# An attention and token-mixer kernel with one fixed order for all engines, a single gelu activation, and plane groups filled by arrival

## The chip, the cores and the metric

The kernel runs on one core of a Trainium2 chip. The metric is the device time of one execution in microseconds (us). A core has engines that run side by side, each through its own list of instructions in order, with semaphores between them: TensorE (PE, matmuls), ScalarE (ACT, activation functions), VectorE (DVE), GpSimd (POOL) and SyncE (SP, which here only issues DMA transfers).

## What is computed

The reference adds three terms over a 2048 x 512 input in bf16:

```python
def _A_ref(x, wqkv, wo):                      # 32 heads of 16 columns
    qkv = ((x @ wqkv).reshape(B, S, 3, H, Dh)).transpose(2, 0, 3, 1, 4)
    q, k, v = qkv[0], qkv[1], qkv[2]
    scores = einsum("bhqd,bhkd->bhqk", q, k) * Dh ** -0.5
    p = softmax(scores, axis=-1)
    o = einsum("bhqk,bhkd->bhqd", p, v)
    return o.transpose(0, 2, 1, 3).reshape(B, S, D) @ wo

def _B_ref(x, w1, b1, w2, b2):                # mixes along the sequence
    h = layernorm(x)
    u = gelu(einsum("bsd,sf->bdf", h, w1) + b1)      # 512 x 1376
    y = einsum("bdf,fs->bds", u, w2) + b2
    return y.transpose(0, 2, 1)

xn = layernorm(x)
return x + _A_ref(xn, ...) + _B_ref(xn, ...)
```

The softmax needs 32 x 2048 x 2048 exponentials, 134 million. They are by far the largest piece of elementwise work.

## The kernel before

**Units.** The attention is cut into 32 blocks (4 blocks of 512 queries by 8 groups of 4 heads). A block has 4 heads, the "rows" r = 0 to 3, and 16 tiles of 128 keys. One head with one key tile is a *unit*: a 128 x 512 tile of scores, 2,048 units in all. A score matmul (`score_mm`, L645) uses a quarter of the PE array's rows, so that up to four scores of four heads run at once into four PSUM banks; such a set is called a *burst*. Seven of the eight PSUM banks hold scores, bank 7 collects the products with V.

**Two ways to the exponential.** An *A unit* is read from PSUM by ScalarE, which computes the exponential (`exp_tile`, L658) over one, two or three neighbouring banks with one instruction, of 512, 1,024 or 1,536 elements for each partition, into a ring of slots (`pT`, and later the space of `wqkv_sb`). A *D unit* is read by VectorE (`dve_first`, L721): it adds a bias to the score as an int16 and clips it, so that the bits of the integer, read as bf16, are a rough power of two. Two shifted copies of these integers, called *planes*, are made by `make_plane` with GpSimd's 64-bit integer add (L730; sometimes with VectorE, L732). The three planes together, weighted, approximate the exponential. An A unit needs one matmul with V (`pv_mm`, L671), a D unit three. Up to four D units of one group lie side by side in one region of 2,048 elements (spare space in `planes`, `x_sb`, `xn_sb`, `xnT` and `w2blk`, whence these names in the profile), and in the kernel before a plane instruction always covers all four places, filled or not, with a place fixed by the row. The program sends 1,378 units by way A and 670 by way D.

**PV matmuls.** They use a quarter of the array's columns each, and up to four of four rows run at once. Below, a *slot* is the time of one such set of up to four matmuls over 512 columns. The QKV, MLP and output projections (L549) have the same form and go in between.

**The rest.** At the end of a block VectorE copies bank 7 out (L1161); for every pair of blocks the denominators go through DRAM to all partitions, with a reciprocal (L1185) and a multiplication (L1204) by VectorE. The token mixer has 11 chains `chain_ut`, one for each 128 columns of w1: 16 matmuls, VectorE's addition of b1 and multiplication by 0.5 (L1058), and then gelu in four steps: square (L1024) and cube (L1028) on VectorE, tanh on ScalarE (L1033), product on VectorE (L1037). Sixteen chains `chain_yo` then multiply with w2 and the output weights. All this is spread over the run between the scores.

**What sets the order.** The order of all engines' instructions is made at build time by a greedy planner: `pe_step` picks the next piece of PE work (a burst, PV matmuls, a step of a chain, or zero matmuls by `z_fill`, L1698) by modelled times of each instruction, `dve_step` and `misc_step` do so for VectorE and GpSimd, and 32 sets of parameters (`STEP_VALUES`), one for each 64 units, steer them. On the chip the order is fixed.

Of the kernel before, what the change touches and what calls it, by code (L numbers as in the profile page):

```python
# [41 lines left out]
def _plane_sum(i):  # L42
    tot = 0.0
    for d, w in zip(SHIFT, WEIGHT):
# [7 lines left out]

DEBUG_SCHED = False
FORM = "P"
N_ZERO0 = 11
N_ZERO1 = 2
N_ZERO2 = 2
NXP = 5
RING_W = 2
W2_POS = 14.2  # L60
DEBUG_CHAINS = False
PLANNED = [0.0]
TUNE0 = dict(even=1, d_end=1, bal=600.0, one_first=False, bal_w=2000.0, lk=0.1, trip=False, marg=60.0, q_max=1400.0, early=0.0, q_lead=1.5, ut=(4.4, 15.28), yo=(15.68, 30.47), d_keep=2, d_last=5, open_pl=2, d_stop=20, w3=1200.0,
            ring_low=4, tol=100.0, lone=800.0, lone_n=2, f_pr=2, f_late=0.2, f_items=3, ring_next=4, pl_next=4, d_slack=120.0,
            pl_open=3, f_bias=0.0, f_early=9.0, s_wait=-1e9, tol2=-1e9, ex2=2.0, ex3=1.0, d_from=1.3, z_cols=3500.0, partial=False, pr_ex=0, dve_planes=6,
            v1=lambda a: (1.2 + 0.8 * a / 16.0, 0.6), v2=lambda a: (2.4 + 1.3 * a / 16.0, 1.6),
            kt=lambda T, c: ((0, 1.0, 2.9, 4.6)[T] + 0.17 * c * (1, 1, 2, 2)[T], (0, 0.5, 2.0, 3.2)[T]))
STEP_KEYS = ("bal", "bal_w", "c_gate", "d_end", "d_from", "d_keep", "d_last", "d_slack", "d_stop", "dve_planes", "early", "even", "ex2", "ex3", "f_bias", "f_early", "f_items", "f_late", "f_pr", "lk", "lone", "lone_n", "marg", "one_first", "open_pl", "partial", "pl_next", "pl_open", "pr_ex", "q_lead", "q_max", "ring_low", "ring_next", "tol", "trip", "z_cols")
STEP_VALUES = (
# [32 lines left out]
)  # L102
STEPS = [dict(zip(STEP_KEYS, v)) for v in STEP_VALUES]
HOOK = [None]
SCORE = (1.05, 0.5, 0.3)
CP_EVERY = 64

GE = "dve"
GELU_C = 0.7978845608028654
NU = 16  # L110
# [1846 lines left out]
```

## Time and profile before

| what | value |
|---|---|
| time, median of 3 runs (lowest to highest) | 671.7 us (671.6 to 671.73) |
| span of the profiled execution (slowest core, the only one) | 670.0 us |
| instructions in the span | 20269 |
| moved by DMA | 30.01 MB |
| DMA queue q1, share of the time of 16 DMA engines | 17.2% |

The profile comes from one execution; its span runs from the first instruction to the last. No total of its own is listed for that execution, so the span is set beside the runs' median. The time of an instruction is the time from its start to its end; neighbours on ScalarE and PE overlap, so the step from one start to the next is shorter than the listed duration, and what an instruction costs its engine is that step.

### The profile page before, as it was taken

Reading aid. Unit: us, or ns where it says so; the run is one execution under the profiler, and the core shown is the slowest. Engines: PE = TensorE matmul, PEld = TensorE weight load, DVE = VectorE, ACT = ScalarE, POOL = GpSimd, SP = SyncE. Lnnn points to the kernel's source line nnn. Section 1 sums busy time; section 2 is a strip of 40 time slices with the busy share of each in tenths; the row PEclk is TensorE's granted clock in tenths of the full one; section 3 lists DMA queues with packets and bytes.
Section 4 is the critical chain, followed back from the end, with each engine's and each line's share of the span. In section 5 each row is a group of like instructions: output and inputs, shape, how many; then the busy total and the mean of one; then the engine's idle time right before and its main releaser. Section 6 shows DMA issues by size and latency. Waiting matters only on the chain.

```text
span 670.0 us, 20269 instructions
## 1 busy us (share of the span) xinstructions
PE 650.3 (97%) x8631; PEld 200.6 (30%) x8631; DVE 582.4 (87%) x970; ACT 654.5 (98%) x830; POOL 490.2 (73%) x511
## 2 busy tenths in 40 slices
PE   8989999999999999999999999999999999999997
PEld 4444333222222222222222222222222223222222
DVE  7886878888998988899888978989898889898895
ACT  6999999999999999999999999999999999999994
POOL 2507558657686779997699786688789678898884
PEclk9999999999999999999999999999999999999999
DMA  7050000201212122010202212122211212211001
GB/s 222 2 109 7 19 20 10 58 12 41 51 38 62 34 50 50 18 42 3 62 26 55 56 45 66 40 48 56 47 35 26 70 31 49 54 41 49 18 21 49
DMA packets 69957, 30.01 MB, mean 45 GB/s; under 512 B 56494, under 2 KB 66734, under 8 KB 69866
## 3 DMA queue, kind: packets, MB, share of 16 engines
q1 hardware_dynamic: 69290, 28.18, 17.2%
q8 instruction: 68, 1.11, 0.7%
q10 hardware_dynamic: 576, 0.52, 0.2%
q14 instruction: 23, 0.19, 0.1%
HBM read 22.15 MB, written 2.61 MB: 37 GB/s over the span
## 4 chain that ended last, share of the span: by engine, by line
ACT 89%; PE 8%; DVE 2%; issue 0%; DVEq 0%
ACT pT L658 64%; ACT wqkv_sb L658 24%; PE ps L645 2%; PE ps L549 2%; PE ps L671 2%; PE ps L555 1%; ACT xres L1033 1%; DVE gT L1037 0%; DVE planes L721 0%; DVE planes L732 0%; PE ps L561 0%; ACT L1033 0%; DVE w2blk L721 0%; ACT mv L517 0%; ACT mv L515 0%
## 5 line engine op out<-in xcount | busy, mean ns | idle before, releaser
L658 ACT ACTIVATE pT<-ps 128x1024 bf16<-128x1024 f32 (+2 forms) x588 | 506.6, 1047 | 1.1 <-PE ps L645 0.7
L645 PE MATMUL ps<-QT,KT 32*128 32x512 bf16 x2048 | 271.5, 384 | 9.6 <-ACT pT L658 4.7
L658 ACT ACTIVATE wqkv_sb<-ps 128x1024 bf16<-128x1024 f32 (+2 forms) x202 | 211.1, 1107 | 0.0
L721 DVE TENSOR_SCALAR planes<-ps 128x512 int16<-128x512 f32 x251 | 165.6, 686 | 23.1 <-PE ps L645 22.2
L721 DVE TENSOR_SCALAR x_sb<-ps 128x512 int16<-128x512 f32 x233 | 154.1, 685 | 24.3 <-PE ps L645 23.5
L671 PE MATMUL ps<-pT,V 128*32 128x512 bf16 x1004 | 169.9, 386 | 1.3 <-DVE V L574 0.8
L645 PEld LDWEIGHTS ps<-QT,KT 32*128 32x128 bf16 x2048 | 75.1, 91 | 270.4 <-ACT pT L658 157.7
L671 PE MATMUL ps<-planes,V 128*32 128x512 bf16 x509 | 93.8, 384 | 0.6 <-DVE planes L732 0.4
L671 PE MATMUL ps<-wqkv_sb,V 128*32 128x512 bf16 x374 | 89.9, 386 | 0.0
L730 POOL INT64_ADD planes<-x_sb x65 | 68.9, 1066 | 26.5 <-DVE x_sb L721 18.2
L721 DVE TENSOR_SCALAR xn_sb<-ps 128x512 int16<-128x512 f32 x99 | 66.1, 686 | 9.3 <-PE ps L645 8.6
L671 PE MATMUL ps<-x_sb,V 128*32 128x512 bf16 x372 | 73.2, 384 | 0.0
L730 POOL INT64_ADD x_sb<-x_sb x41 | 44.1, 1079 | 36.4 <-DVE x_sb L721 33.2
L730 POOL INT64_ADD planes<-planes x56 | 59.6, 1068 | 11.6 <-DVE planes L721 11.5
L730 POOL INT64_ADD x_sb<-planes x49 | 52.4, 1073 | 16.6 <-DVE planes L721 13.7
L671 PE MATMUL ps<-planes,V17b 128*32 128x512 bf16 x251 | 62.2, 384 | 0.0
L671 PE MATMUL ps<-x_sb,V17b 128*32 128x512 bf16 x233 | 60.9, 385 | 0.1
L549 PE MATMUL ps<-xn_sb,w1blk 128*32 128x512 bf16 x688 | 58.4, 383 | 0.2 <-DVE qraw L935 0.2
L549 PE MATMUL ps<-gT,w2blk 128*32 128x512 bf16 (+1 forms) x704 | 57.5, 383 | 0.2 <-ACT pT L658 0.2
L671 PEld LDWEIGHTS ps<-pT,V 128*32 128x32 bf16 x1004 | 43.2, 94 | 46.0 <-issue 35.7
L721 DVE TENSOR_SCALAR xnT<-ps 128x512 int16<-128x512 f32 x65 | 42.7, 684 | 3.5 <-PE ps L645 3.2
L671 PE MATMUL ps<-xn_sb,V 128*32 128x512 bf16 x209 | 44.6, 384 | 0.0
(114 smaller groups left out, 897.3 us busy)
## 6 DMA issues: line engine op xcount, KB each, us to landing
w1blk<-in_B_w_dram SPq DMA_DIRECT2D x10, 512.0 KB, 4.4
w2blk<-in_B_w_dram SPq DMA_DIRECT2D x16, 320.0 KB, 3.4
denb<-rec_scr SPq DMA_DIRECT2D x16, 256.0 KB
xres<-in_A_x_dram SPq DMA_DIRECT2D x16, 128.0 KB, 2.3
QT<-qraw SPq DMA_DIRECT2D x120, 16.0 KB, 1.8
OT<-OT SPq DMA_DIRECT2D x60, 32.0 KB, 2.0
out_dram<-osb SPq DMA_DIRECT2D x13, 128.0 KB, 1.8
x_sb<-in_A_x_dram SPq DMA_DIRECT2D x2, 512.0 KB, 7.1
```

What stands on the lines that cost most here:

```text
L549: op = sc.add("pe", lambda e, sl=sl, c=c: e.matmul(dst[sl, :], lhsT=lhsT[:, sl], rhs=rhs, start=start, stop=stop, tile_position=(0, 32 * c ...
L555: return sc.add("pe", lambda e: e.matmul(bank(bk)[:, 0:n], lhsT=zer[:, 512:640], rhs=zer[:, 0:n], start=True, stop=True), reads=[("zer",)] ...
L645: return sc.add("pe", lambda e: e.matmul(bank(bk), lhsT=KT[32 * r:32 * r + 32, T, 128 * kt:128 * (kt + 1)], rhs=QT[32 * r:32 * r + 32, slo ...
L658: return sc.add("act", lambda e: e.activation(slots(us), pick(ps3, bs), ACTF.Exp, scale=EXP_SCALE), reads=[("bank", b) for b in bs], write ...
L671: return sc.add("pe", lambda e: e.matmul(bank(PV_BANK)[32 * r:32 * r + 32, :], lhsT=vt_[:, off:off + 32], rhs=rhs, start=start, stop=stop, ...
L721: return sc.add("dve", lambda e: e.tensor_scalar(plane_i[pb][:, 512 * r:512 * (r + 1)], bank(bk), BIAS + SHIFT[0], float(SHIFT[0]), ALU.ad ...
L730: return sc.add("pool", lambda e: e.int64_add(plane_q[pb], plane_q[pb0], -down * LANES), reads=rd, writes=wr, name="plane", occ=1015.0, la ...
L1033: return sc.add("act", lambda e: e.activation(gB[0:m, :], gB[0:m, :], ACTF.Tanh, scale=2.0 * GELU_C * GC), reads=kB, writes=kB, occ=t["occ ...
```

## The change

**The order.** The planner, its cost model and its parameters are gone. A text constant, `ORDER`, some 21,400 characters long, lists in one sequence what is issued: `C` the next step of a chain, `S` a burst with its units, banks and, for D units, plane region, `E` an exponential, `F` a D unit's first plane, `L` a further plane, `P` a set of PV matmuls, `Z` zero matmuls, `U` work of the tail. `replay` reads it and adds the instructions to the engines' lists. So how many units go each way, how wide the exponentials are and what stands next to what is now set by the table. Counted from the two programs:

| | before | after |
|---|---|---|
| A units / D units | 1,378 / 670 | 1,327 / 721 |
| exponentials of 512 / 1,024 / 1,536 | 217 / 558 / 15 | 90 / 611 / 5 |
| groups of D units | 228 | 308 |
| GpSimd 64-bit adds | 453, all 1,024 wide | 616: 216 of 256, 126 of 512, 122 of 768, 152 of 1,024 |
| planes by VectorE (L732) | 3 | 0 |
| bursts of scores | 640 | 642 |
| sets of PV, zero and chain matmuls over 512 columns | 1,406 | 1,417 |
| zero matmuls, quarters (L1698, now L1075) | 61 | 15 |

The widths of the adds are those of the 32-bit view that the order lists print; 1,024 is all four places of a group.

**Gelu.** The chains end with the addition of b1 (L958, without the factor 0.5). When all 11 are done, `gelu_all` runs ScalarE's gelu in the tanh form over 10 of the tiles with one instruction (128 x 5120, L964), and over the last one with another (96 x 512, L966), in place in `gT`. The 33 VectorE steps and 11 tanh activations are gone. There are two more loads of an activation table in the run instead of one: to gelu, and back to the exponential.

**Groups.** A D unit takes the next free place of its group, whatever its row, and `make_plane` covers only the places that are filled. The planes' memsets at the start (five regions and `w2blk`), which gave unfilled places a value, are gone.

```diff
+ORDER = """
+C006C00C00S3000011025E20EL2C00S3032103114EA3EH5Z7C00C1NC011C01C01C01C01C01S3045056060C1NEM6E18C01C1TC01C01C01C01C01C01
...
         def late_consts():
...
-            z += [lambda j=j: memset("pool", pl_flat.bitcast(F32)[:, 1024 * j:1024 * (j + 1)], 0.0,
-                                     [("pl", j, r) for r in range(4)], 900) for j in range(NXP)]
-            z += [lambda: memset("pool", w2_flat.bitcast(F32)[:, 0:1024], 0.0, [("pl", P_W2, r) for r in range(4)], 900)]
...
-        def make_plane(eng, j, pb0, pb):
+        def make_plane(eng, j, pb0, pb, n):
             down = SHIFT[0] - SHIFT[j]
-            rd = [("pl", pb0, r) for r in range(4)]
-            wr = [("pl", pb, r) for r in range(4)]
+            rd = [("pl", pb0, r) for r in range(n)]
+            wr = [("pl", pb, r) for r in range(n)]
             if eng == "pool":
-                return sc.add("pool", lambda e: e.int64_add(plane_q[pb], plane_q[pb0], -down * LANES),
+                return sc.add("pool", lambda e: e.int64_add(plane_q[pb][:, 0:128 * n], plane_q[pb0][:, 0:128 * n],
+                                                               -down * LANES),
...
-        def gelu_steps(ft, m):
...
-            return [Step(GE, sq, 650), Step("dve", cube, 650), Step("act", tanh, 480), Step("dve", mul, 650)]
...
+            def ev(bk):
+                sc.add("dve", lambda e: e.tensor_scalar(gT[0:m, ft, :], bank(bk)[0:m, :], b1f[0:m, ft:ft + 1], None, ALU.add),
+                    [("bank", bk), ("b1f",)], [("gT", ft)])
...
+        def gelu_all(bk):
+            ks = [("gT", ft) for ft in range(NFTF)]
+            sc.add("act", lambda e: e.activation(gT[:, 0:NFTF, :], gT[:, 0:NFTF, :], ACTF.Gelu_apprx_tanh), ks, ks)
+            ks = [("gT", NFTF)]
+            sc.add("act", lambda e: e.activation(gT[0:MLAST, NFTF, :], gT[0:MLAST, NFTF, :], ACTF.Gelu_apprx_tanh), ks, ks)
...
+        def replay(text):
...
+                elif k == "L":
+                    e_, p0 = divmod(num(), 32)
+                    pb = num()
+                    made[p0] += 1
+                    closed[p0] = True
+                    make_plane("dve" if e_ else "pool", made[p0], p0, pb, len(group[p0]))
+                    for sl, (b, kt, r) in enumerate(group[p0]):
+                        item[b, kt, r, made[p0]] = (plane_b[pb][:, 512 * sl:512 * (sl + 1)], ("pl", pb, sl), 0)
...
+        replay(ORDER)
```

Three places show how the instructions stand. The lists give line, operation, written tile and, after the arrow, read tile, with the shape; a count at the end says how many alike follow each other.

First ScalarE where the kernel before does its first tanh, in the middle of exponentials; the other ten follow further on:

```order
L658 ACTIVATE pT<-ps 128x1024 x2
L658 ACTIVATE pT<-ps 128x512
L658 ACTIVATE pT<-ps 128x1024
L658 ACTIVATE pT<-ps 128x512
L1033 ACT_TABLE_LOAD
L1033 ACTIVATE xres<-xres 128x512
L658 ACTIVATE pT<-ps 128x1024
L658 ACTIVATE pT<-ps 128x512
```

And ScalarE in the changed kernel around its one gelu, near the middle of the run:

```order
L725 ACTIVATE pT<-ps 128x1024 x2
L725 ACTIVATE pT<-ps 128x512
L725 ACTIVATE wqkv_sb<-ps 128x512
L964 ACT_TABLE_LOAD
L964 ACTIVATE gT<-gT 128x5120
L966 ACTIVATE gT<-gT 96x512
L725 ACT_TABLE_LOAD
L725 ACTIVATE pT<-ps 128x512
L725 ACTIVATE wqkv_sb<-ps 128x512
L725 ACTIVATE pT<-ps 128x1024
```

The eleven single activations have become one stretch without an exponential, between two table loads.

VectorE in the kernel before, from the addition of b1 of one chain (L1058) on, with first planes of D units (L721) in several regions:

```order
L1058 TENSOR_SCALAR gT<-ps,b1f 128x512
L1185 RECIPROCAL den<-den 128x32
L721 TENSOR_SCALAR x_sb<-ps 128x512 x2
L1024 TENSOR_TENSOR osb<-gT 128x512
L721 TENSOR_SCALAR x_sb<-ps 128x512 x2
L1028 SCALAR_TENSOR_TENSOR xres<-osb,gT 128x512
L721 TENSOR_SCALAR x_sb<-ps 128x512
L721 TENSOR_SCALAR planes<-ps 128x512
L1037 SCALAR_TENSOR_TENSOR gT<-xres,gT 128x512
```

And VectorE in the changed kernel from the addition of b1 of a chain (L958) on:

```order
L958 TENSOR_SCALAR gT<-ps,b1f 128x512
L787 TENSOR_SCALAR xnT<-ps 128x512 x4
L787 TENSOR_SCALAR planes<-ps 128x512 x6
L787 TENSOR_SCALAR x_sb<-ps 128x512
L1038 RECIPROCAL den<-den 128x32
L787 TENSOR_SCALAR x_sb<-ps 128x512
L787 TENSOR_SCALAR w2blk<-ps 128x512 x4
```

Where three gelu steps of a chain stood between D units, only D units and the steps of the denominators are left.

GpSimd, a stretch of planes in the kernel before, all of full width:

```order
L730 ISA xnT<-planes 128x1024
L730 ISA planes<-planes 128x1024
L730 ISA x_sb<-x_sb 128x1024 x2
L730 ISA xnT<-xn_sb 128x1024
L730 ISA planes<-xn_sb 128x1024
```

And in the changed kernel:

```order
L796 ISA xnT<-planes 128x512
L796 ISA planes<-xnT 128x256 x2
L796 ISA planes<-xn_sb 128x1024
L796 ISA xn_sb<-xn_sb 128x1024
L796 ISA x_sb<-x_sb 128x1024 x2
L796 ISA planes<-x_sb 128x1024
```

Groups of one or two units are now cut to the width that is filled, and there are more of them.

More of the change, by code (lines that the diff above doesn't have):

```diff
@@ L51 @@
 BIAS = 127.0 * 128.0 - 128.0 * float(np.log2(0.5 * (min(_RATIO) + max(_RATIO))))
-DEBUG_SCHED = False
-FORM = "P"
 N_ZERO0 = 11
 N_ZERO1 = 2
-N_ZERO2 = 2
 NXP = 5
+NU = 16
 RING_W = 2
[L60 to L69, printed above, removed]
[32 rows of a table removed]
[L102 to L110, printed above, removed]
 NQS = 4
@@ L131, in __init__ @@
         self.after = None
-        self.name = name
-        self.start = 0.0
-        self.occ = 0.0
-        self.end = 0.0
-SWITCH = 95.0
-TICK = 3413.3
-TICK_COLS = 3060.0
 class Sched:
@@ L563, in transpose_pe @@
                     xn_sb[:, t, ct * 128:(ct + 1) * 128], ident[:]),
-                    reads=[("xn", t)] + [("ident", q) for q in range(4)], writes=[("bank", bk)], cfg="F", n=128)
+                    reads=[("xn", t)] + [("ident", q) for q in range(4)], writes=[("bank", bk)])
             return op
@@ L579, in transpose_copy @@
             src = ps_bf[:, bk * 1024: bk * 1024 + 512 * n_].rearrange("p (t ct j) -> p t ct j", t=n_, ct=NCT)
-            return copy(eng, dst, src, [("bank", bk)], [("xnT", t) for t in range(t0_, t0_ + n_)], 512 * n_, 1.8)
+            return copy(eng, dst, src, [("bank", bk)], [("xnT", t) for t in range(t0_, t0_ + n_)])
         def kt_mm(T, t0_, n_, ct, bk, off=0):
@@ L658, in exp_tile, with pv_mm @@
             return sc.add("act", lambda e: e.activation(slots(us), pick(ps3, bs), ACTF.Exp, scale=EXP_SCALE),
-                          reads=[("bank", b) for b in bs], writes=[("pT", u) for u in us], name="exp", extra_deps=slot_deps(us),
-                          occ=427.0 * w + 50.0, lat=427.0 * w + 248.0)
-        def pv_mm(b, kt, r, rhs, rkey, which, start, stop, last):
+                          reads=[("bank", b) for b in bs], writes=[("pT", u) for u in us], extra_deps=slot_deps(us))
+        def pv_mm(b, kt, r, rhs, rkey, which, start, stop):
             qb, G, T, e_ = blk_of(b)
@@ L894, in chain_kt @@
-        def chain_kt(T, t0_, n_, due, rel, eng="dve"):
-            ch = Chain("kt%d.%d" % (T, t0_), [], due, rel, gate=lambda: all(t in xT_ok for t in range(t0_, t0_ + n_)))
-            def fin():
-                op = kt_evac(T, t0_, n_, ch.bk[0], eng)
-                kt_ok.update((T, t) for t in range(t0_, t0_ + n_))
-                return op
-            ch.steps = [Step("pe", lambda ct=ct: kt_mm(T, t0_, n_, ct, ch.bk[0]), 226) for ct in range(NCT)]
-            ch.steps.append(Step(eng, fin, 610, frees=True))
-            return ch
@@ new lines, in v_steps, with b1_steps, const_steps, last @@
+        def v_steps(t, n_, T0_, T1_):
+            n = 128 * (T1_ - T0_)
+            return [lambda bk, i=i, ct=ct: v_mm(t + i, T0_, T1_, ct, bk, n * i) for i in range(n_) for ct in range(NCT)] + [
+                lambda bk: v_evac(t, n_, T0_, T1_, bk, "dve"), lambda bk: v_scale(t, n_, T0_, T1_)]
+        def b1_steps():
+            return [lambda bk: b1_turn(bk),
+                    lambda bk: copy("dve", b1f[:, :], ps_bf[:, bk * 1024:bk * 1024 + NFT], [("bank", bk)], [("b1f",)])]
+        def const_steps():
+            fs = late_consts()
+            def last(bk):
+                fs[-1]()
+                memset("dve", gT[96:97, NFT - 1, :], 1.0, [("gT1",)])
+            return [lambda bk, f=f: f() for f in fs[:-1]] + [last]
@@ L932, in ev @@
                 rb[0] = n_q[0] % 2
                 n_q[0] += 1
-                q_done[qb] += 1
-                return vec("dve", lambda e, k=rb[0]: e.tensor_scalar(qraw[:, k, :], bank(ch.bk[0]), QSCALE, None, ALU.mult),
-                           [("bank", ch.bk[0])], [("qraw", rb[0])], 512)
-            def ok():
-                return consts_ok[0] and all(not any(row_left[bb]) for bb in (b0 - 4, b0 - 3) if bb >= 0)
+                sc.add("dve", lambda e, k=rb[0]: e.tensor_scalar(qraw[:, k, :], bank(bk), QSCALE, None, ALU.mult),
+                    [("bank", bk)], [("qraw", rb[0])])
@@ L977, in chain_late @@
-        def chain_late():
-            steps = [lambda i=i: ld_b1(i) for i in range(2)]
-            steps += [lambda ft=ft: w1_load(ft) for ft in range(NW1)]
-            steps += [ld_wo] + [lambda e_=e_, r=r: ld_wop(e_, r) for e_ in range(2) for r in range(4)]
-            ch = Chain("late", [], 90.0, 0.0, ex=False)
-            def one(f):
-                f()
-                return None
-            ch.steps = [Step("sp", lambda f=f: one(f), 600, gate=lambda: pos() > 1.0 and consts_ok[0]) for f in steps]
-            return ch
@@ L989, in chain_w2 @@
-        def chain_w2():
-            ch = Chain("w2", [], 90.0, 0.0, ex=False)
-            ch.steps = [Step("sp", yt_next, 600, gate=lambda: pos() >= W2_POS and P_W2 not in pl_busy) for _ in range(NW2)]
-            return ch
+                    dma("sp", QT[p0:p0 + 16, slot, :], qraw[p0:p0 + 16, rb[0], :], reads=[("qraw", rb[0])],
+                        writes=[("QT", slot, r)])
+            return [lambda bk, ct=ct: qt_mm(qb, T, ct, bk) for ct in range(NCT)] + [
+                ev, lambda bk: spread(0), lambda bk: spread(1)]
@@ L1063, in chain_ut, with ev @@
-            ch.steps.append(Step("dve", ev, 650, frees=True))
-            ch.steps += gelu_steps(ft, m)
-            return ch
-        def yt_mm(ch, st, ft, first, last):
+            def ev(bk):
+                sc.add("dve", lambda e: e.tensor_scalar(gT[0:m, ft, :], bank(bk)[0:m, :], b1f[0:m, ft:ft + 1], None, ALU.add),
+                    [("bank", bk), ("b1f",)], [("gT", ft)])
+            return [lambda bk, st=st: mm(st, bk) for st in range(NT)] + [ev]
+        def gelu_all(bk):
[3 more added lines that the diff above has]
+            sc.add("act", lambda e: e.activation(gT[0:MLAST, NFTF, :], gT[0:MLAST, NFTF, :], ACTF.Gelu_apprx_tanh), ks, ks)
@@ L1115, in chain_yo @@
-            if not lastqb:
-                for T in range(4):
-                    ch.steps.append(Step("pe", lambda T=T: op_mm(qb, sti, T, ch.bk[0], False, T == 3), 226))
-                def fin():
-                    op = vec("dve", lambda e: e.tensor_tensor(osb[:, ob, :], bank(ch.bk[0]), xres[:, ob, :], ALU.add),
-                             [("bank", ch.bk[0]), ("xres", ob)], [("osb", ob)], 512)
-                    store(st, ob)
-                    yo_done[qb] += 1
-                    return op
-                ch.gate = lambda: len(oT_done[qb]) == NG and gelu_done[0]
-            else:
-                def fin():
-                    op = vec("dve", lambda e: e.tensor_tensor(part[:, sti, :], bank(ch.bk[0]), xres[:, ob, :], ALU.add),
-                             [("bank", ch.bk[0]), ("xres", ob)], [("part", sti), ("w1blk", 0), ("w1blk", 1)], 512)
-                    part_done[0] += 1
-                    return op
-                ch.gate = lambda: gelu_done[0]
@@ L1151, in chain_epi, with yt, fin @@
-        def chain_epi(b):
+            def yt(ft, bk):
+                if ft == 0:
+                    dma("sp", xres[:, ob, :], x2[128 * st:128 * (st + 1), :], reads=[], writes=[("xres", ob)])
+                yt_mm(bk, st, ft, ft == 0, lastqb and ft == NFT - 1)
+            z = [lambda bk, ft=ft: yt(ft, bk) for ft in range(NFT)]
+            if not lastqb:
+                z += [lambda bk, T=T: op_mm(qb, sti, T, bk, False, T == 3) for T in range(4)]
+                def fin(bk):
+                    sc.add("dve", lambda e: e.tensor_tensor(osb[:, ob, :], bank(bk), xres[:, ob, :], ALU.add),
+                        [("bank", bk), ("xres", ob)], [("osb", ob)])
+                    dma("sp", out2[128 * st:128 * (st + 1), :], osb[:, ob, :], reads=[("osb", ob)], writes=[("out", st)],
+                        out_dma=True)
+            else:
+                def fin(bk):
+                    sc.add("dve", lambda e: e.tensor_tensor(part[:, sti, :], bank(bk), xres[:, ob, :], ALU.add),
+                        [("bank", bk), ("xres", ob)], [("part", sti), ("w1blk", 0), ("w1blk", 1)])
@@ L1301, in take @@
-        def take(b, kt, r, kind):
-            row_left[b][r].remove(kt)
-            while row_blk[r] < NBLK and not row_left[row_blk[r]][r]:
-                row_blk[r] += 1
-            n_assigned[0] += 1
-            items_left[b][r] += 1 if kind == "A" else NPL
-        def kv_done():
-            if not kv_ok[0] and len(kt_ok) == 4 * NKT and len(v_ok) == 4 * NKT:
-                kv_ok[0] = True
-                for u in range(U_X, U_X + N_UX):
-                    ring_free[u] = True
-            return kv_ok[0]
@@ L1344, in plane_release @@
-        def plane_release(j):
-            pl_busy[j] -= 1
-            if pl_busy[j] == 0:
-                del pl_busy[j]
-        BK = tuple(range(7))
-        def free_banks(t):
-            z = [(sc.ready(writes=[("bank", k)]), k) for k in BK if k not in dbanks and k not in ex_bank]
-            return [k for v, k in sorted(z) if v <= t]
-        def d_backlog(t):
-            return max(0.0, sc.free["dve"] - t) + 600.0 * len(dbanks)
-        def runs_of(v, w):
-            return [tuple(range(a, a + w)) for a in sorted(v) if all(a + i in v for i in range(w))]
@@ L1570, in issue_d @@
-        def issue_d(ds, i, n):
-            new = None
-            for r, u, k, g in ds:
-                if g == "new":
-                    new = new or d_open()
-                    g = new
-                g["slots"][r] = u
-                nd_row[u[0]][r] += 1
-                take(u[0], u[1], r, "D")
-                op = score_mm(u[0], u[1], r, k, i == n - 1)
-                i += 1
-                dbanks[k] = (op, g, r, u)
-                n_d[0] += 1
-                g["n0"] += 1
-                if g in cur_pl and all(z is not None for z in g["slots"]):
-                    d_close(g)
@@ new lines, in bass_parallel_sum__softmax_full_mha__mixer_token_mlp__prompt_kernel, with zero_rows @@
+        n_banked = len(chains)
+        chains += [st_steps(a) for a in range(4, NT, 2)] + [[lambda bk, t=t: ln_norm(t)] for t in range(4, NT)]
+        chains += [[lambda bk: ln2_scales()], late_steps(), [lambda bk: w2_load()] * 2, const_steps()]
+        chains += [[lambda bk, t=t: ln2_norm(t)] for t in range(NT)] + [[gelu_all]]
+        chains += [epi_steps(b) for b in range(NBLK - 1)]
+        def zero_rows(bk, rows, starts, stop):
+            for r in rows:
+                sc.add("pe", lambda e, r=r: e.matmul(
+                    bank(bk)[32 * r:32 * r + 32, :], lhsT=zer[:, 512:544], rhs=zer[:, 0:512],
+                    start=r in starts, stop=stop, tile_position=(0, 32 * r)),
+                    reads=[("zer",)], writes=[("bank", bk)])
```

1377 lines of the change are left out of this document (415 added, 962 removed), and 32 rows, old and new, of the table STEP_VALUES.

## The prediction

> **What bounds the kernel now.** I read the shares of busy time first, then the chain of work that ended last, then the busy time in stretches of 20 us from 20 to 640 (31 of them; the emptiest and the two fullest neighbours for PE, and the sum). The columns of the stretches are length, then PE, weight loads, VectorE, ScalarE, GpSimd busy (instructions), the granted PE clock, DMA share, GB/s.
>
> ```profile
> span 670.0 us, 20269 instructions
> PE 650.3 (97%) x8631; PEld 200.6 (30%) x8631; DVE 582.4 (87%) x970; ACT 654.5 (98%) x830; POOL 490.2 (73%) x511
> ...
> ACT 89%; PE 8%; DVE 2%; issue 0%; DVEq 0%
> ```
>
> ```profile
> 300.00:320.00 20.00, 19.58 (x234) 5.72 (x226) 18.15 (x29) 19.68 (x30) 14.58 (x13) 1.00 0.02 5
> ...
> 440.00:460.00 20.00, 20.00 (x262) 5.61 (x266) 18.23 (x30) 20.00 (x23) 16.37 (x16) 1.00 0.22 56
> 460.00:480.00 20.00, 20.00 (x264) 5.63 (x261) 18.63 (x31) 20.00 (x24) 16.59 (x16) 1.00 0.15 39
> ...
> sum 620.00, PE 608.76 PEld 184.60 DVE 544.72 ACT 618.59 POOL 467.69; mean PE 19.64 PEld 5.95 DVE 17.57 ACT 19.95 POOL 15.09
> ```
>
> PE and ScalarE both look full, but the chain belongs to ScalarE (89%), and ScalarE is without work for only 1.4 of 620 us. PE's 97% is stretched: its matmuls wait for banks that ScalarE has still to empty, as the largest wait of its weight loads says (total, times, longest).
>
> ```profile
> PEld ps L645 <- ACT pT L658: 157.7, 374, 1.3
> ```
>
> So the sum of ScalarE's work sets the time, and whatever comes off it comes off the span, until another engine is as long.
>
> **ScalarE's sum.** The groups by shape (count | busy, mean ns):
>
> ```profile
> L658 ACT ACTIVATE pT<-ps 128x1024 bf16<-128x1024 f32 x398 | 412.8, 1168 | 0.6 <-PE ps L645 0.3
> L658 ACT ACTIVATE wqkv_sb<-ps 128x1024 bf16<-128x1024 f32 x160 | 179.3, 1178 | 0.0
> L658 ACT ACTIVATE pT<-ps 128x512 bf16<-128x512 f32 x181 | 113.6, 754 | 0.5 <-PE ps L645 0.3
> L658 ACT ACTIVATE wqkv_sb<-ps 128x512 bf16<-128x512 f32 x36 | 25.9, 722 | 0.0
> L658 ACT ACTIVATE pT<-ps 128x1536 bf16<-128x1536 f32 x9 | 14.6, 1623 | 0.0
> L658 ACT ACTIVATE wqkv_sb<-ps 128x1536 bf16<-128x1536 f32 x6 | 9.2, 1528 | 0.0
> ```
>
> Neighbours overlap, so I take steps from start to start, from ScalarE's timeline (start, duration):
>
> ```profile
> 10.68 2.92 ACT L658 ACTIVATE pT<-ps 128x512 bf16<-128x512 f32 x4
> ...
> 134.02 1.28 ACT L1033 ACT_TABLE_LOAD   x1
> 135.31 0.63 ACT L1033 ACTIVATE xres<-xres 128x512 f32<-128x512 f32 x1
> ...
> 312.30 0.75 ACT L658 ACTIVATE wqkv_sb<-ps 128x512 bf16<-128x512 f32 x1
> 312.78 0.78 ACT L1033 ACTIVATE xres<-xres 128x512 f32<-128x512 f32 x1
> 313.30 3.08 ACT L658 ACTIVATE pT<-ps 128x1024 bf16<-128x1024 f32 x4
> ...
> 321.70 2.99 ACT L658 ACTIVATE pT<-ps 128x1024 bf16<-128x1024 f32 x3
> 324.41 2.11 ACT L658 ACTIVATE wqkv_sb<-ps 128x1024 bf16<-128x1024 f32 x2
> ...
> 437.04 1.45 ACT L658 ACTIVATE wqkv_sb<-ps 128x1536 bf16<-128x1536 f32 x1
> 438.39 1.94 ACT L658 ACTIVATE pT<-ps 128x1024 bf16<-128x1024 f32 x2
> ...
> 658.23 2.86 ACT L658 ACTIVATE pT<-ps 128x512 bf16<-128x512 f32 x4
> ```
>
> A step is 0.48 us for 512 elements (312.78 - 312.30), 0.904 for 1,024 ((324.41 - 321.70)/3), 1.33 to 1.35 for 1,536, 0.52 for a tanh (313.30 - 312.78), 1.29 for a table load. Exponentials before: 558 x 0.904 + 217 x 0.477 + 15 x 1.331 = 627.9 us. The first starts at 10.68, the last ends at 661.09: 650.4 us, of which 11 tanh take 5.7, the load 1.3, and 15.5 are left for the layer norm's small activations and waits, most of it in the first and the last block.
>
> After: 611 x 0.904 + 90 x 0.477 + 5 x 1.331 = 601.9, **26.0 us less**. Of this, 23.0 come from 51 units that go to VectorE (0.452 each), 3.0 from wider instructions. The tanh go: **-5.7**. Gelu over 10 tiles has no row. A further 512 elements cost an exponential 0.427 (0.904 - 0.477), so 10 x 0.427 + 0.05 + 0.48 for the last tile gives 4.8; at tanh's 0.52 a tile, 11 tiles would take 5.7. I take the first, since one instruction covers ten tiles: **+4.8**, with 5.7 as the other end. One more table load: **+1.3**.
>
> The next instruction after the load of before starts 1.29 us later, so the row shows no more than the load. The Trainium skill ("ScalarE: Activation LUTs", section "What ACT_TABLE_LOAD costs") gives some 1,380 ns of drain besides, 2.66 us for each switch. By that the two switches would cost 5.3 instead of 2.6 and the forecast would be 2.7 us later; the row speaks against it, unless the drain falls on the wait before the load.
>
> **What the others have to bear.** PE's steps come from its timeline:
>
> ```profile
> 308.49 0.39 PE L645 MATMUL ps<-QT,KT 32*128 32x512 bf16 x3
> 308.81 0.39 PE L671 MATMUL ps<-pT,V 128*32 128x512 bf16 x1
> ...
> 309.47 0.38 PE L671 MATMUL ps<-pT,V 128*32 128x512 bf16 x1
> ...
> 309.79 0.39 PE L645 MATMUL ps<-QT,KT 32*128 32x512 bf16 x2
> ```
>
> A burst to the first PV set takes 0.32 us, a PV set to the next 0.22 ((309.47 - 308.81)/3; 0.216 over longer runs), the last PV set to a burst 0.32. 51 more D units add 102 PV matmuls; 46 zero matmuls go; all in all 11 more sets (+2.4 us) and 6 more switches (6 x 0.42 = +2.5). At these steps PE's work is 607 us before and 611 after, against ScalarE's 643 and 617. VectorE: gelu's 33 steps go, 51 first planes come.
>
> ```profile
> L1024 DVE TENSOR_TENSOR osb<-gT 128x512 f32<-128x512 bf16 x10 | 10.5, 1049 | 0.0
> L1028 DVE SCALAR_TENSOR_TENSOR xres<-osb,gT 128x512 f32<-128x512 f32 x10 | 10.4, 1040 | 0.1
> L1037 DVE SCALAR_TENSOR_TENSOR gT<-xres,gT 128x512 bf16<-128x512 f32 x10 | 9.3, 928 | 2.2 <-ACT xres L1033 2.1
> ...
> 321.36 0.68 DVE L1161 COPY OT<-ps 128x512 f32<-128x512 f32 x1
> 321.96 1.28 DVE L721 TENSOR_SCALAR xnT<-ps 128x512 int16<-128x512 f32 x2
> ```
>
> A PSUM operation has a step of 0.60 (321.96 - 321.36): 51 x 0.60 = 31 us in, some 27 out (the gelu groups by their steps), 541 to 547 in sum. Off the path on average.
>
> By stages of 64 scores, with these steps on both programs' lists: in the 30 middle stages ScalarE's sum goes from 586.0 to 561.6, PE's from 552.0 to 553.5, VectorE's from 488 to 487. Before, ScalarE was longest in each. After, PE exceeds it slightly in a dozen, so that the longest engines add up to 563.5: +1.9. In the first stage VectorE has 38.3 against ScalarE's 36.8 (+1.5), in the last 21.5 against 19.1 (+2.4, of which 1.3 existed before). **+4.4 net**; below it, 0, if neighbouring stages even out.
>
> Is PE's idle time real slack? The 27 stretches from 100 to 640 hold 251 PE instructions on average (234 at 300:320), and the changed kernel would need some 261. The fullest rows above hold 262 and 264, with ScalarE busy for all 20.00 us. So PE has shown the pace, though for tens of us and not for all.
>
> The gelu pauses exponentials for 7.4 us with its loads. In that stage the list gives VectorE 12 or 13 D units to empty banks meanwhile, at 0.60 each, and PE 21.8 us of work against 22.9: the pause is hidden from PE. If that cover failed, PE would stand still for up to 5 us, but ScalarE's own sum has the pause in it already.
>
> **GpSimd.** 453 full adds become 616 of four widths, 1,442 filled places instead of 1,812. No partial add has a row.
>
> ```profile
> L730 POOL INT64_ADD planes<-x_sb x65 | 68.9, 1066 | 26.5 <-DVE x_sb L721 18.2 <-PE ps L645 8.3
> ...
> 287.88 1.04 POOL L730 INT64_ADD xnT<-planes  x1
> 288.89 1.04 POOL L730 INT64_ADD x_sb<-planes  x1
> ...
> L420 POOL MEMSET planes<- 128x1024 f32 x5 | 4.9, 1023 | 0.0
> ...
> L424 POOL MEMSET jrow<- 128x1 f32 x32 | 1.0, 98 | 0.3 <-POOLq L1942 0.3
> ```
>
> A memset of one element takes 0.1 us and of 1,024 takes 1.02, so GpSimd's fixed part is about 0.1. With a full add's step of 1.01 (288.89 - 287.88) the new sum is 616 x 0.1 + 1,442 x 0.228 = 390 us: less than the 459 now, and hidden. The other end, width costing nothing, is a rival below. The memsets that go (6 us) lie in a stretch where GpSimd waited anyway: nothing.
>
> **Sum**, on the span of the profiled execution: 670.0 - 26.0 - 5.7 + 4.8 + 1.3 + 4.4 = 648.8 us. The runs' median lies 1.7 above that span, so **650.5 us**, 3.2% less than 671.7.
>
> **Rivals.**
> *PE takes over.* If PE's idle before (650 - 607 = 43 us) is the price of handing banks back and forth, it stays. In full: 671.7 + 4 for its added work, some 675.5, no gain; with half of that loss, about 663. For: both sums are now within 1.4% in the middle, and a burst needs its bank freed, whoever frees it. Against: ScalarE's rows at 20.00. Chance 0.18 for 656 to 668, 0.04 for the full price.
>
> *GpSimd becomes the bound (slower).* An add costs 1.01 whatever its width: 616 x 1.014 = 625 us of planes, which start at about 45 us and leave some 10 after them: about 680. It decides once the fixed part of an add exceeds 0.77 us, where GpSimd's middle stages (364 us without a fixed part, about 256 more at 1.014) reach ScalarE's 561.6. PV sets would then wait for planes. Against it the memset rows, for it that this add is no memset. Chance 0.05.
>
> *The clock.* 46 zero matmuls fewer could let PE fall to a lower clock. Cold matmuls at the start take 0.44 each (4.87/11) where a set takes 0.216 later:
>
> ```profile
> 1.24 4.87 PE L555 MATMUL ps<-zer 128*128 128x512 bf16 x11 [1.24 <-DVE zer L420]
> ```
>
> Granted clock is 1.00 in all rows above, and PE gets denser. A few lapses of 3 to 4 us at half pace would cost 1.7 each: 655. Chance 0.03.
>
> *The change does more than priced.* Of the 15.5 us of waits and small work some 3 go with the new order of the first and the last block, and the +4.4 vanishes: 641 to 645. Chance 0.07.
>
> **How the numbers follow.** Forecast 645 to 656: 0.63. Rivals as above. The range 642 to 665 leaves out the full price of PE (0.04), GpSimd (0.05) and the outer parts of the two neighbours (about 0.05). Faster by over 0.2% (what a measurement here can tell from no change): 0.63 + 0.18 + 0.03 + 0.07 = 0.91. The full price of PE is halved between same, 0.02, and slower, 0.02, and GpSimd's 0.05 makes slower 0.07.
>
> **What would show it.** ScalarE's exponentials at the same steps and 701 + 5 of them; gelu at 4.3 + 0.5 with two loads of 1.28 and no gap; ScalarE at 20.00 in the stretches, PE with some 261 instructions; GpSimd's mean add near 0.63. It would be wrong if ScalarE shows idle time released by PE scores in the middle (PE's rival), if a 256 add takes near 1 us (GpSimd's), or if clock rows fall below 1.00.

## The result and the profile after

The changed kernel takes 709.3 us (median; 709.17 to 709.4) against 671.7 of the kernel before: a ratio of 1.0559, with a 95% interval of 1.0544 to 1.0573. It is **5.6% slower**, where 3.2% less had been forecast. The span of its profiled execution is 707.6 us.

The page of the changed kernel, its busy shares and the head of the chain that ended last:

```profile
span 707.6 us, 20485 instructions
PE 664.1 (94%) x8687; PEld 205.0 (29%) x8687; DVE 582.6 (82%) x985; ACT 642.9 (91%) x738; POOL 423.1 (60%) x668
...
PE 58%; DVE 20%; POOL 16%; ACT 3%; issue 2%; DMA 0%; POOLq 0%; DVEq 0%
```

Every engine's share has fallen. ScalarE, which had 89% of the chain, has 3%; VectorE and GpSimd, which had 2% between them, have 36%, though neither is busy for a larger share of the span than before. So no engine's sum of work sets this time: the chain runs from one engine to the next. The same stretches as before:

```profile
300.00:320.00 20.00, 19.96 (x265) 5.99 (x265) 18.45 (x30) 20.00 (x24) 14.03 (x18) 1.00 0.05 15
...
440.00:460.00 20.00, 18.74 (x234) 5.52 (x234) 16.82 (x27) 18.17 (x21) 14.12 (x22) 1.00 0.15 37
460.00:480.00 20.00, 19.49 (x242) 5.13 (x234) 17.44 (x29) 18.99 (x21) 14.00 (x22) 1.00 0.19 49
```

At 300 to 320 the new order does what was forecast, 265 PE instructions with ScalarE full. In most other stretches from 60 to 660 us ScalarE is busy for 17 to 19.5 of 20 us; in the kernel before it never fell below 19.6 between 40 and 640. The waits say on whom. In the kernel before (engine, what for; us in total, times, longest):

```profile
PEld ps L671 <- POOL planes L730: 2.6, 11, 0.5
PEld ps L671 <- POOL x_sb L730: 1.2, 5, 0.3
PEld ps L671 <- POOL xn_sb L730: 0.8, 4, 0.2
ACT pT L658 <- PE ps L645: 0.7, 2, 0.3
PEld ps L671 <- POOL xnT L730: 0.4, 2, 0.2
```

In the changed kernel:

```profile
ACT pT L725 <- PE ps L712: 36.3, 60, 1.3
PEld ps L737 <- POOL planes L796: 32.4, 68, 1.4
PEld ps L737 <- POOL x_sb L796: 23.2, 48, 1.0
PEld ps L737 <- POOL xn_sb L796: 15.6, 28, 1.1
PEld ps L737 <- POOL xnT L796: 12.0, 23, 1.0
ACT wqkv_sb L725 <- PE ps L712: 11.5, 23, 1.0
PE ps L737 <- POOL planes L796: 9.1, 25, 0.9
PEld ps L737 <- POOL w2blk L796: 3.5, 6, 1.0
```

PE's weight loads for PV matmuls wait 86.7 us for GpSimd's planes, 173 times (before: 5.0 us, 22 times), and ScalarE waits 47.8 us for scores, 83 times (before: 0.7 us). A weight load can wait while PE still works on earlier matmuls, so not all of the 86.7 us is lost: PE's matmuls themselves stand still for planes for 28.9 us, 76 times, summed over the five tiles that hold planes (before: 0.2 us, once). One such case, from the timeline of the changed kernel:

```profile
164.95 0.47 PE L712 MATMUL ps<-QT,KT 32*128 32x512 bf16 x4
165.33 0.82 POOL L796 INT64_ADD xnT<-planes  x1
...
165.64 0.38 PE L737 MATMUL ps<-planes,V17b 128*32 128x512 bf16 x1
...
166.13 0.40 POOL L796 INT64_ADD w2blk<-x_sb  x1
166.21 0.39 PE L737 MATMUL ps<-xnT,V 128*32 128x512 bf16 x1 [0.19 <-POOL xnT L796]
...
166.50 2.05 POOL L796 INT64_ADD planes<-x_sb  x3
166.76 0.39 PE L712 MATMUL ps<-QT,KT 32*128 32x512 bf16 x4
...
167.19 1.02 ACT L725 ACTIVATE pT<-ps 128x1024 bf16<-128x1024 f32 x1 [0.38 <-PE ps L712]
```

GpSimd writes a plane into `xnT` from 165.33 to 166.15. The PV set that reads it could start at 165.86, one set after 165.64, but starts at 166.21, 0.35 us late. The next burst stands behind it on PE, and comes at 166.76. ScalarE, which had nothing else in a bank, is idle for 0.38 us. The wait for a plane has become a wait of ScalarE.

From the two traces, the time between the end of each add and the first PV matmul that reads it: a median of 1.71 us before and 0.58 after, and under 0.12 us (PE was waiting) for 13 of 453 planes before and 176 of 616 after. That is the new order's doing, not GpSimd's speed, whose groups by shape show shorter adds than before (630 ns in the mean for this one, where 1066 stood):

```profile
L796 POOL INT64_ADD planes<-x_sb x101 | 62.9, 630 | 29.6 <-DVE x_sb L787 21.6 <-PE ps L737 4.0 <-PE ps L617 3.9
```

### The profile page after: what moved, and what is told of

Read it like the earlier page. It is cut to its first block, busy times and chain, and to the rows that moved or that the text cites. A ratio compares the mean times of both kernels' runs of the same rounds, so it can differ in the third digit from the quotient of the medians.

```text
span 707.6 us, 20485 instructions
## 1 busy us (share of the span) xinstructions
PE 664.1 (94%) x8687; PEld 205.0 (29%) x8687; DVE 582.6 (82%) x985; ACT 642.9 (91%) x738; POOL 423.1 (60%) x668
## 4 chain that ended last, share of the span: by engine, by line
PE 58%; DVE 20%; POOL 16%; ACT 3%; issue 2%; DMA 0%; POOLq 0%; DVEq 0%
PE ps L737 22%; PE ps L712 20%; PE ps L617 16%; POOL planes L796 6%; POOL x_sb L796 5%; DVE planes L787 5%; DVE x_sb L787 4%; DVE xn_sb L787 3%; POOL xn_sb L796 3%; ACT pT L725 2%; POOL xnT L796 2%; DVE OT L1022 1%; DVE xnT L787 1%; DVE stats L577 1%; POOL w2blk L796 1%
## 5 line engine op out<-in xcount | busy, mean ns | idle before, releaser
L725 ACT ACTIVATE pT<-ps 128x1024 bf16<-128x1024 f32 (+1 forms) x524 | 475.4, 987 | 38.0 <-PE ps L712 36.3
L712 PE MATMUL ps<-QT,KT 32*128 32x512 bf16 x2048 | 258.5, 385 | 2.2 <-ACT pT L725 0.9
L725 ACT ACTIVATE wqkv_sb<-ps 128x1024 bf16<-128x1024 f32 (+2 forms) x182 | 181.1, 1023 | 12.4 <-PE ps L712 11.5
L737 PE MATMUL ps<-pT,V 128*32 128x512 bf16 x974 | 179.0, 387 | 0.0
L712 PEld LDWEIGHTS ps<-QT,KT 32*128 32x128 bf16 x2048 | 67.2, 91 | 235.5 <-ACT pT L725 102.8
L737 PE MATMUL ps<-planes,V 128*32 128x512 bf16 x555 | 122.7, 387 | 10.3 <-POOL planes L796 9.1
L737 PE MATMUL ps<-x_sb,V 128*32 128x512 bf16 x425 | 95.8, 386 | 8.0 <-POOL x_sb L796 7.2
L737 PE MATMUL ps<-planes,V17b 128*32 128x512 bf16 x257 | 72.9, 385 | 0.0
L787 DVE TENSOR_SCALAR xnT<-ps 128x512 int16<-128x512 f32 x91 | 60.2, 685 | 15.0 <-PE ps L712 14.5
L737 PE MATMUL ps<-xnT,V 128*32 128x512 bf16 x199 | 49.6, 389 | 4.6 <-POOL xnT L796 4.2
```

Source lines behind the costliest of these rows:

```text
L712: return sc.add("pe", lambda e: e.matmul(bank(bk), lhsT=KT[32 * r:32 * r + 32, T, 128 * kt:128 * (kt + 1)], rhs=QT[32 * r:32 * r + 32, slo ...
L725: return sc.add("act", lambda e: e.activation(slots(us), pick(ps3, bs), ACTF.Exp, scale=EXP_SCALE), reads=[("bank", b) for b in bs], write ...
L737: return sc.add("pe", lambda e: e.matmul(bank(PV_BANK)[32 * r:32 * r + 32, :], lhsT=vt_[:, off:off + 32], rhs=rhs, start=start, stop=stop, ...
L787: return sc.add("dve", lambda e: e.tensor_scalar(plane_i[pb][:, 512 * r:512 * (r + 1)], bank(bk), BIAS + SHIFT[0], float(SHIFT[0]), ALU.ad ...
```

## The experiments

Three theories: **A**, PE stands in line behind planes that are not ready, and ScalarE starves behind it; **B**, PE is full, and its work with the handing back of banks takes the time; **C**, the single gelu stretch does it. Each run stands beside runs of the kernel before on the same chip: 671.7 us for the first four rows, 672.2 for the next three, 671.7 for the last two.

| run | us | ratio to before (95%) |
|---|---|---|
| adds over half the columns | 672.5 | 1.0007 (0.9997 to 1.0018) |
| adds over all four places | 883.5 | 1.315 (1.313 to 1.317) |
| without gelu | 709.3 | 1.0562 (1.0546 to 1.0577) |
| tokens re-sorted, first | 670.2 | 0.9979 (0.9969 to 0.9989) |
| tokens re-sorted, with margins | 657.8 | 0.9791 (0.9776 to 0.9806) |
| kernel before, gelu of the change | 691.5 | 1.0287 (1.0269 to 1.0304) |
| kernel before, adds cut | 671.9 | 0.9995 (0.9986 to 1.0004) |
| re-sorted with margins, without gelu | 659.4 | 0.9817 (0.9801 to 0.9834) |
| tokens re-sorted, transfers at 4.8 us | 656.5 | 0.9775 (0.9761 to 0.979) |

**Shorter adds.**

```diff
-                return sc.add("pool", lambda e: e.int64_add(plane_q[pb][:, 0:128 * n], plane_q[pb0][:, 0:128 * n],
+                return sc.add("pool", lambda e: e.int64_add(plane_q[pb][:, 0:64 * n], plane_q[pb0][:, 0:64 * n],
```

> The changed kernel, with each of GpSimd's 64-bit adds over half of the filled columns only (the second half of both shifted planes is not computed, the memsets of the planes are back so that they hold zeros). Its steps fall from 0.37 to 1.01 us to about 0.27 to 0.59. Theory A (PE stands still at PV sets whose planes GpSimd has not finished, and ScalarE starves behind it): planes come early enough, about 671 us instead of 709. Theory B (PE is full: its work and the handing back of banks take the time, whatever the planes do): no change to speak of, 700 or more. Theory C (the single gelu stretch with its table loads costs the time): 709.

672.5 us: 36.8 us come back when nothing but GpSimd's adds gets shorter (the memsets at the start only add work), on an engine that was busy for 60% of the span. Theory B falls: PE's work was the same. Planes are now waited for 44.3 us in all instead of 86.7, and ScalarE waits 15.6 us for scores instead of 47.8. The largest of these waits:

```profile
PEld ps L742 <- POOL planes L801: 17.2, 52, 1.0
ACT pT L730 <- PE ps L717: 12.9, 33, 1.5
PEld ps L742 <- POOL x_sb L801: 10.7, 32, 0.6
```

**Longer adds**, that is the cut to filled places undone.

```diff
-                return sc.add("pool", lambda e: e.int64_add(plane_q[pb][:, 0:128 * n], plane_q[pb0][:, 0:128 * n],
-                                                               -down * LANES),
+                return sc.add("pool", lambda e: e.int64_add(plane_q[pb], plane_q[pb0], -down * LANES),
```

> The changed kernel, with the cut of the adds to the filled places undone: every add takes all four places again (memsets of the planes back too), 616 adds of 1.01 us = 625 us in all. Unfilled places may overwrite data of another group, so the output need not be the reference's. Theory A: every group of one or two units gets its planes 0.4 to 1.3 us later, PE waits for them in line, and the time goes far beyond GpSimd's own 625 + some 55 at the ends: about 860 us. Theories B and C: GpSimd stays shorter than the run, so 709 to 720.

883.5 us. GpSimd is busy for 645.5 of the 881.5 us of this span and heads the chain:

```profile
PE 743.3 (84%) x8687; PEld 211.8 (24%) x8687; DVE 593.1 (67%) x985; ACT 655.6 (74%) x738; POOL 645.5 (73%) x674
...
POOL 42%; PE 35%; DVE 15%; issue 6%; ACT 1%; DMA 0%; POOLq 0%; DVEq 0%; SPq 0%
```

Some 220 us more of adds cost 174 us, though the engine has 236 us without work: what counts is the delay at each PV set, not the sum. (The 23 us above the expectation may come from PE's granted clock, 0.926 on average in this run, whose PE stands still more often; that was not tested. The edit also makes an add wait for the places that are not filled, which was not tested apart either.) With its order, the change depends on the narrow adds.

**No gelu.**

```diff
         def gelu_all(bk):
-            ks = [("gT", ft) for ft in range(NFTF)]
-            sc.add("act", lambda e: e.activation(gT[:, 0:NFTF, :], gT[:, 0:NFTF, :], ACTF.Gelu_apprx_tanh), ks, ks)
...
+            return
```

> The changed kernel without gelu: both activations and their two table loads are left out, the MLP goes on with the sums before gelu; everything else stays in its place. This takes 7.4 us off ScalarE. Theory C: 702 or less, if the stretch upsets its surroundings far less. Theories A and B: ScalarE has idle time near by, 708 to 709.

709.28 us against 709.26. Theory C falls: 7.4 us taken off ScalarE bring nothing here.

**The same tokens in another order.** The search simulated the engines with the steps of the traces and kept every token's bank, ring place and plane region, so that all instructions are the same, apart from which PV matmul of a head comes first and one zero matmul more. Only the text changes, here its first line:

```diff
-C006C00C00S3000011025E20EL2C00S3032103114EA3EH5Z7C00C1NC011C01C01C01C01C01S3045056060C1NEM6E18C01C1TC01C01C01C01C01C01
+C006C00S3000011025S3032103114E20C00C00Z7C1NEL2C011C01C01C01C01EA3C01C00C01C01C01C01C1OS3045056060EH5C01C01C01C01C01C01
```

> The changed kernel with another ORDER: the same 4,684 tokens, each with its bank, ring place and plane region as before, sorted anew so that PV sets stand behind other PE work until their planes are there. The sequence was found with a small model of the five engines that uses the steps and the delays between engines of the trace after; it gives 696 us for the order of the change and 660 for the kernel before, 1.5% below the spans measured in both, and 644 for this one. Theory A: about 656 us, with the same instructions. Theory B: PE's work is the same, so little can be won, 700 or more. Theory C: 700 or more, gelu is the same.

670.2 us: 39 us less than the change, a bare 0.2% below the kernel before, and 14 more than expected. Two stretches of this run lost most, where ScalarE has about 4 us less work than in the first row here (columns as before; the number after GpSimd's is the granted PE clock):

```profile
480.00:500.00 20.00, 19.43 (x250) 5.70 (x250) 18.78 (x30) 19.62 (x22) 15.77 (x24) 1.00 0.14 39
500.00:520.00 20.00, 17.64 (x183) 4.20 (x175) 14.35 (x25) 15.22 (x17) 10.77 (x16) 0.83 0.23 55
...
580.00:600.00 20.00, 17.16 (x209) 5.03 (x207) 13.53 (x23) 15.69 (x18) 11.56 (x18) 0.91 0.22 57
```

And its timeline at the first of the two, with the clock behind it:

```profile
507.39 0.53 SPq L482 DMA_DIRECT2D den_scr<-OT  x1
...
507.97 2.42 SPq L485 DMA_DIRECT2D OT<-OT  x4
...
510.43 0.59 SPq L482 DMA_DIRECT2D den<-den_scr  x1
...
510.88 0.39 PE L707 MATMUL ps<-QT,KT 32*128 32x512 bf16 x2
...
512.49 0.35 DVE L1033 RECIPROCAL den<-den 128x32 f32<-128x32 f32 x1 [3.20 <-DMA den<-den_scr]
512.76 1.22 DVE L782 TENSOR_SCALAR xn_sb<-ps 128x512 int16<-128x512 f32 x2
...
513.44 1.19 PE L707 MATMUL ps<-QT,KT 32*128 32x512 bf16 x2 [2.17 <-DVE xn_sb L782]
```

```profile
514.00:516.00 2.00, 2.00 (x13) 0.46 (x16) 1.98 (x4) 0.24 (x1) 1.68 (x3) 0.50 0.09 18
516.00:518.00 2.00, 2.00 (x19) 0.24 (x11) 1.18 (x3) 1.51 (x2) 2.00 (x4) 0.50 0.63 186
```

The reciprocal now came too early for its transfers, each of which holds SyncE's queue for 0.53 to 0.61 us here. VectorE stood 3.2 us, the D units behind it kept their banks, PE stood 2.2 us, and then ran at half clock, 0.50, from 513 to 519. The same illness, with another pair of engines.

**With margins for those transfers**, the order searched again.

> Again the changed kernel with its tokens sorted anew, this time with the transfers of the denominators as the last run showed them: each holds SyncE's queue for 0.5 to 0.65 us and lands 2.0 us after its issue (the model behind the former order let them pass in 0.06), and with some margin on the way from VectorE to GpSimd. The model gives 641 us, with 1.5% on top 651 for the span. Theory A (waits in line, on planes and now on the denominators, are what is lost; where they are gone, the stalls of PE and its half clock go too): about 653 us. Theory B (PE is full): not below the 670 of the former order by more than 3.

657.8 us, 12 less, so PE was not full at 670; it is 5 more than expected. In the profiled execution, of 659.3 us, one wait of 2.3 us for denominators remained, behind a load of w1, with PE at half clock for 3.4 us after it. The other three took 657.6 to 657.8 us, at a granted clock of 0.999 to 1.000.

**The parts of the change on the kernel before.** The gelu alone, as a step of its own for the planner:

```diff
-            ch.steps += gelu_steps(ft, m)
...
+        bg.append(chain_gelu())
```

> The kernel before, with the gelu of the change alone: the planner places one activation over 10 tiles and one over the last as soon as all 11 sums are there. Counted: 1,414 A units instead of 1,378 (243, 551 and 23 exponentials of 512, 1,024 and 1,536), since the parameters were set for the other gelu. If sums of work decided, 627.9 becomes 645 us of exponentials: some 15 us more, 688. The model of the engines gives 678 against 660, hence 690. If the single gelu were a gain as such, 670 or less.

691.5 us. Of the 243 activations of 512 that the expectation counts, two are copies into `xnT`, so there are 1,412 A units. The kernel is 19 us slower since its planner, with parameters set for other work, gives ScalarE more to do: at the steps above the 34 more units make 15.8 us, and exponentials between the two gelu instructions make four table loads of 1.28 us out of one, 3.8 us. ScalarE is busy for 675.0 us instead of 654.5, idle for 14.9 instead of 15.5, and has 91% of the chain. So in the planner's order the sum of ScalarE's work does set the time. This run does not show what the gelu alone would be worth.

The adds alone, cut behind the last filled place:

```diff
-                op = make_plane(eng, j, g["pl"][0], pb)
+                op = make_plane(eng, j, g["pl"][0], pb, 1 + max(r for r in range(4) if g["slots"][r] is not None))
```

> The kernel before, with the adds cut behind the last filled place (334 of 453 stay full, 16, 35 and 68 become 256, 512 and 768 wide), order untouched. Theory A: its PV sets stand 1.7 us (median) behind their planes, so nothing waits on them: 671.7, no change. Were GpSimd's own time on the path of the kernel before, some us less.

671.9 us against 672.2 on that chip, no change: where PV sets stand well behind their planes, shorter adds are worth nothing.

**The re-sorted kernel without gelu.**

> The re-sorted kernel of the run with margins (657.8 us), without gelu: both activations and their two table loads left out, the MLP goes on with the sums before gelu. If ScalarE's sum sets the time there, as the prediction had it, 7.4 us less: about 650. If PE does (its chain has 67% of the span there against ScalarE's 21%), and ScalarE's pause is hidden behind VectorE's D units, no change within 1: 657 to 658. The model of the engines says no change.

659.4 us, 1.6 more and so outside the 657 to 658 expected, though the intervals of the two ratios overlap. In any case 7.4 us less of ScalarE's work bring nothing: even here its pause lies beside work of others, and its sum does not set the time.

**A third order**, with 4.8 us for each transfer in the search.

> The tokens sorted anew a third time, with 4.8 us for every transfer in the search, since the last order still waited 2.3 us for one transfer of denominators behind a load of w1 (at 126 us), after which PE stood for 1.8 us and ran at half clock for 3.4. The model, with the transfers as usual, gives 643.0 us against 641.2 for the former order, so by it alone 1.9 us more, 659.7. If the wait and the half clock it brought are gone, about 4 less: 655 to 656. So 655 to 660; below 657 speaks for the half clock as a real loss, 659 to 660 against it.

656.5 us, the lowest, 2.3% below the kernel before and 7.4% below the change. Its ratio's interval overlaps that of the run with margins, whose other executions had no lapse of the clock to speak of, so this run does not settle what a lapse costs. Its page and the waits that answer to those above:

```profile
span 654.8 us, 20533 instructions
PE 638.8 (98%) x8688; PEld 203.3 (31%) x8688; DVE 577.6 (88%) x985; ACT 633.3 (97%) x738; POOL 423.0 (65%) x668
...
PE 58%; ACT 31%; DVE 8%; POOL 2%; issue 1%; DMA 1%; DVEq 0%; POOLq 0%; SPq 0%
```

```profile
PEld ps L732 <- POOL x_sb L791: 5.2, 18, 0.6
ACT pT L720 <- PE ps L707: 3.8, 10, 0.5
PEld ps L732 <- POOL planes L791: 3.3, 13, 0.4
```

Its granted clock is 1.00 throughout. With the instructions of the change, planes are waited for 13.4 us in all instead of 86.7, and its PV sets start a median of 1.14 us after their planes.

## Why the prediction was wrong

**What held.** ScalarE's bound in the kernel before, and the counts and steps: exponentials at 0.904 us, gelu at 4.47 us for ten tiles where 4.3 was priced, three table loads of 1.28. From ScalarE's timeline of the changed kernel:

```profile
332.48 1.28 ACT L964 ACT_TABLE_LOAD   x1
333.78 4.47 ACT L964 ACTIVATE gT<-gT 128x5120 bf16<-128x5120 bf16 x1
```

Gelu starts 1.30 us after the start of its load, and the exponential before the load ends at 332.46, 0.02 us ahead of it. By the Trainium skill ("ScalarE: Activation LUTs", section "What ACT_TABLE_LOAD costs") a switch has 1.38 us of drain besides; the trace shows none. GpSimd's fixed part is 0.16 us, where 0.1 had been taken from the memsets: steps of 0.37, 0.59, 0.80 and 1.01 for the four widths, 406 us in all against 390. And the sum itself was nearly what these instructions cost without waits in line: 650.5 forecast, 656.5 measured for the best order. That is in part luck: the forecast took ScalarE's sum to be the limit, and in the re-sorted kernel 7.4 us less of ScalarE's work changed nothing.

**What failed: that GpSimd's work, being less, was "hidden".** The paragraph compared its sum, 390 us, with the span and dropped it. The time that PE and ScalarE stand in line for planes was put at nothing. For no single plane was it asked how long after its last score it can be there, and where in PE's list the set that reads it stands. The distance had shrunk from 1.71 to 0.58 us in the median, and in place of a hidden GpSimd the runs show PE standing still for planes for 28.9 us and ScalarE waiting 47.8 us for scores behind it; 53 us come back when the same instructions stand in another order. Counting stages of 64 scores could not see this, since a PE that stops for 0.35 us at a set has the same sum of work. The evidence lay in the order of the two kernels: the model that the expectations name gives 660 and 696 from the two lists, a ratio of 1.055 where 1.0559 was measured. It was made afterwards, though, with the steps and delays of the changed kernel's trace; whether those of the trace before would have done was not tried.

**The rivals.** "GpSimd becomes the bound" named the right wait, PV sets waiting for planes, but tied it to GpSimd's total and to adds whose cost does not fall with width; they do fall, and the wait came all the same, at 60% of busy time. The run with full adds shows the price of that condition on top: 883 rather than the 680 forecast from sums. "PE takes over" was not the cause, as the run with shorter adds and the re-sorted ones show; in the best order PE has 58% of the chain and ScalarE 31%, so there it may be about half true, and may hold the 6 us between 650.5 and 656.5. That was not tested apart.

**The clock.** It was 0.997 on average here, with one lapse to half clock of 3.4 us, from 682.6, small beside 38 us. Longer lapses showed in the first re-sorted run. By the Trainium skill ("TensorE: Matmul & The Clock Gate", Part 1: The HAM clock gate) half clock comes after an idle window of about 3.4 us; in the first re-sorted run a stop of 2.2 us was enough.

**Sizes.** The measured span is 58.8 us above the forecast one, 648.8. ScalarE was idle ahead of exponentials for 50.4 us in 123 places (before: 1.1 us in 7), of which 47.8 are the waits for scores. An exponential that starts after a pause does not overlap the one before it (1.02 instead of 0.904 us), which by an estimate makes 116 x 0.12 = 14 more. Beyond what the kernel before had, that is 63 us; the forecast held 4.4 of it, for the stages in which another engine is longer, and the rest is 59.

**Gelu.** Its terms (-5.7, +4.8, +1.3) were right as work and worth nothing as time: taking it out made neither the changed kernel nor the re-sorted one faster.

What stays open: for which durations the order of the change was made. With adds of half the length it comes back to 672.5 us; which figures it was found with, no trace shows.

## What to carry to other kernels

A fixed order on engines that take their lists in turn is only as good as the distance between each result and the instruction that reads it. Before trusting sums of work, run the new lists through measured steps with their waits; here a small model of that kind gave the sign and the size, though with steps of the new trace. Where a table is searched off line, give each hand-over a margin, those through DMA above all, and look at waits with a short total but many times: each of them stops all that stands behind it.

## What was not expected of the hardware

In the first re-sorted run, a PE that stopped for 2.2 us ran at half clock for more than the next 6, so a wait can cost more than its length; after a stop of 2.8 us in the same run and one of 1.8 us in the run with margins it was 3.4 us. The small transfers of the denominators hold SyncE's queue 0.53 to 0.61 us each in the timeline above, so that four of them delay a fifth by 2.4. The 64-bit add costs 0.16 us and 0.21 for each place (the steps of 0.37, 0.59, 0.80 and 1.01). An engine's result reaches the next engine after 0.04 us (PE to ScalarE), 0.05 (GpSimd to PE), and 0.10 or 0.17 (VectorE to GpSimd): the least gaps between end and start in the two traces, and for the last pair the two values around which they lie.
